# Sparse attention and a feed-forward layer on one core: batch 0's local q and k are cast and turned in halves, in a new order

## The chip, the cores and the metric

One core of a Trainium2 chip. The metric is the device time of one execution in microseconds (us). The kernel is bound to one core, so its time is that core's. Times inside the run are counted from the start of the profiled span.

## The reference

Eight batches of eight heads, 576 tokens, 64 numbers per head. Heads 0 to 3 attend to a local window of 32 earlier tokens, heads 4 to 7 to earlier tokens of the same residue modulo 32. The attention output, as 4608 rows of 512, goes through a feed-forward layer of width 2048 with a leaky slope of its own per column:

```python
rel = pos[:, None] - pos[None, :]
mask_local = (rel >= 0) & (rel < stride)          # stride = 32, heads 0..3
mask_strided = (rel >= 0) & (pos[None, :] % stride == pos[:, None] % stride)   # heads 4..7
attn = softmax(where(mask, q @ k.T / sqrt(D), -1e9))
x = (attn @ v).transpose(0, 2, 1, 3).reshape(B * S, H * D)
h = x @ w_in
out = (max(h, 0) + alpha * min(h, 0)) @ w_out
```

## The kernel before, in words

**Pairs.** Heads are worked on two at a time. A batch has four pairs: 0 and 1 are the local heads, 2 and 3 the strided heads; pair g of the whole run belongs to batch g // 4. For each pair the kernel computes scores (the two heads' 64 rows on the two halves of the partitions), exponentials on ScalarE, the product with v (which has a column of ones, so that the row sum comes with it), a reciprocal and a multiplication on VectorE, and transposes of the result into xT, the input of the first linear layer (line 585), which works on 512 tokens at a time in 16 pieces of 128 columns of w_in.

**Batch 0's stage.** Before line 585 can run at full length, batch 0's four pairs have to be through. This stage is written out by hand as a list of steps (lines 837 to 842), and `keep` holds every instruction in program order on its engine. The queues are in order: a step that waits holds back whatever stands behind it on the same engine. The steps:

- `warm(17)`, `w(1)`: matmuls of 512 columns on zeros, whose result nobody reads (lines 759 to 762).
- `F(nm, pr)` (`turn_first`, 146 to 158): the strided q or k of pair 2 + pr, as loaded, is transposed in two banks of four; ScalarE evicts the first, VectorE the second.
- `Sc(g, i)` (`score_piece`, 275 to 322): half i of pair g's scores, 6 or 8 short matmuls and two that add the mask, then the exponentials on ScalarE, in one instruction (i = 0, tile sp) or two (i = 1, two banks of tag "hps").
- `vs(0, pr)` (`cast_v`): VectorE copies the strided v of two heads into place. `alpha`: a small transpose and VectorE's 1 - alpha.
- `Cl(0, nm)` (`cast_l`, 177 to 180): POOL casts the local q or k (128 x 1152) from float32 to float16, all nine tokens of a partition at once.
- `T(0, nm)` (`transpose_piece`, 254 to 273): nine transposes into two banks (five and four tokens), each evicted into qT or kT: for q both by ScalarE, for k the second by VectorE.
- `Pv(g, a)` (`pv_piece`, 390 to 418): piece a of pair g's product with v, then a reciprocal (line 413) and a multiplication (line 415) on VectorE. A strided pair has three pieces (6, 6 and 4 blocks), a local pair two of 6.
- `X(g)` (`x_piece`, 428 to 440): pair g's result is transposed and evicted into xT, by ScalarE for a strided pair and VectorE for a local one, if nothing else is said.
- `ov(0, eng, c0, c1)` (`over_v`): copies the 32 rows of overlap in the local v, half on POOL, half on VectorE; the local Pv read them.
- `L(m)` (`lin1_piece` with `begin`, 573 to 590): the first two of the four matmuls of piece m of line 585, those that need pairs 2 and 3 only.

After the list come loads for batch 1, issued on POOL's and SP's queues, and the loop over the 16 pieces of line 585 (854 to 858); pieces 0 to 3, which were begun, need only the matmuls for pairs 0 and 1.

**Buffers.** PSUM has three buffers of tag "ps" (used by F, alpha, T, Pv and X in turn, and by some pieces of line 585), three of tag "hps" (one holds the warm matmuls' result until the last of them, the others serve the scores and line 585), and the two banks of sp. A buffer is free again when its last reader is done.

Of the kernel before, what the change touches and what calls it, by code (L numbers as in the profile page):

```python
# [10 lines left out]
F16 = mybir.dt.float16  # L11
# [21 lines left out]
def kernel(  # L33
# [10 lines left out]
    nc = tc.nc  # L44
    keep = tc.keep_in_program_order
# [11 lines left out]
    hpool = ctx.enter_context(tc.tile_pool(name="half", bufs=4))  # L57
# [5 lines left out]
    pspool = ctx.enter_context(tc.tile_pool(name="ps", bufs=3, space=bass.MemoryType.PSUM))  # L63
# [10 lines left out]
    ident = consts[:, 0:128]  # L74
# [10 lines left out]
    qTs = [cpool.tile([128, 2, 672], F16, name=f"qT{i}") for i in range(2)]  # L85
    kTs = [cpool.tile([128, 2, 672], F16, name=f"kT{i}") for i in range(2)]
# [7 lines left out]
    loaded = {}  # L94
    cast16 = {}
# [50 lines left out]
    def turn_first(nm, pr):  # L146

        t32 = loaded[(nm, pr)]
        dst = (qTs if nm == "q" else kTs)[1].rearrange("r e c -> r (e c)")
        for h in range(2):  # L150
            tp = pspool.tile([128, 512], F32, tag="ps", name="tf")
            for j in range(4):
                keep(nc.tensor.transpose(
                    tp[:, 72 * j : 72 * j + 72], t32[:, 512 * h + 128 * j : 512 * h + 128 * j + 128], id32))
            c0 = 320 * (2 * pr + h)
            cast_copy(("act", "dve")[h],
                      dst[:, c0 : c0 + 320].rearrange("r (j p) -> r j p", p=80)[:, :, 0:72],
                      tp[:, 0:288].rearrange("r (j p) -> r j p", p=72))
# [18 lines left out]
    def cast_l(b, nm, eng="pool"):  # L177
        t16 = hpool.tile([128, 9, 2, 64], F16, tag=f"{nm}l16", bufs=2, name=f"{nm}l16")
        cast_copy(eng, t16, loaded[(b, False, nm)].rearrange("p f (t d) -> p t f d", t=9))
        cast16[(b, False, nm)] = t16  # L180

    def load_v(b, strided):


        if strided:
            st = spool.tile([128, 2048], F16, tag="v", bufs=2, name="stv")
            step = 2 if b == 0 else 4
            for h in range(0, 4, step):
                keep(nc.gpsimd.dma_start(
                    st[0:72, 512 * h : 512 * (h + step)].rearrange("p (h e) -> p h e", h=step),  # L190
                    v[b, 4 + h : 4 + h + step, :, :].rearrange("h (p t) d -> p h (t d)", t=8)))
            loaded[b] = st
        else:
            v16 = vls[b % 2]
            base = v[b, 0:1, 0:1, :]
            r0 = 32 if b < 2 else 0
            step = 12 if b == 0 else 24
            for c in range(0, 24, step):
                keep(nc.gpsimd.dma_start(
                    v16[r0:128, c : c + step, 0:64],  # L200
                    bass.AP(tensor=base.tensor, offset=base.offset + (96 * c - 32 + r0) * D,
                            ap=[[D, 128 - r0], [96 * D, step], [1, D]])))
            cast16[(b, False, "v")] = v16

    def cast_copy(eng, o, i):
        if eng == "act":
            keep(nc.scalar.copy(o, i))
        elif eng == "dve":
            keep(nc.vector.tensor_copy(o, i))
        else:  # L210
            keep(nc.gpsimd.tensor_copy(o, i))  # L211
# [42 lines left out]
    def transpose_piece(u, nm):  # L254

        b = u // 2  # L260
        early = b < NEARLY
        src = cast16[(b, False, nm)]
        dst = qTs[u % 2][:, :, 0:576] if nm == "q" else kTs[u % 2][:, :, 32:608]
        o = dst.rearrange("r e (p t) -> r e p t", t=9)
        tps = []
        for t0, t1 in ((0, 5), (5, 9)):
            tp = pspool.tile([128, 8, 64, 2], F16, tag="ps", name="tp")
            for t in range(t0, t1):
                keep(nc.tensor.transpose(
                    tp[:, t - t0].rearrange("r p e -> r (p e)"), src[:, t].rearrange("p f d -> p (f d)"), ident))  # L270
            tps.append(tp[:, 0 : t1 - t0].rearrange("r t p e -> r e p t"))
        cast_copy("act", o[:, :, :, 0:5], tps[0])
        cast_copy("dve" if early and (u or nm == "k") else "act", o[:, :, :, 5:9], tps[1])
# [116 lines left out]
    def pv_piece(P, a):  # L390
        while defer and any(P.et[z][0] is defer_et["et"] for z in P.et):
            defer.pop(0)()
        if P.x16 is None:
            if P.xd and P.strided:
                P.x16 = x16s
            else:
                P.x16 = xpool.tile([128, 1024], F16, tag="x16", name="x16")
        v16 = cast16[(P.b, P.strided, "v")]
        grp = P.pgroups[a]
        r = 72 if P.strided else 128  # L400
        pv = pspool.tile([128, 512], F32, tag="ps", name="pv")
        nb = 2 * len(grp)
        for x in range(nb):
            t, hh = grp[x // 2], x % 2
            et, c = P.et[(t, hh)]
            keep(nc.tensor.matmul(  # L406
                pv[:, 65 * x : 65 * x + 65], et[0:r, c : c + 128],
                v16[0:r, 2 * P.pr + hh, t, :] if P.strided else v16[:, 6 * (2 * P.pr + hh) + t, :],
                start=(x == 0), stop=(x == nb - 1), skip_group_check=True))
        w = P.w  # L410
        rc = rpool.tile([128, 8], F32, tag="rc", name="rc")
        pvv = pv[0:w, 0 : 65 * nb].rearrange("r (c e) -> r c e", e=65)
        keep(nc.vector.reciprocal(rc[0:w, 0:nb], pvv[:, :, 64]))  # L413
        c0 = 128 * grp[0]
        keep(nc.vector.tensor_tensor(  # L415
            P.x16[0:w, c0 : c0 + 64 * nb].rearrange("r (c e) -> r c e", e=64),
            pvv[:, :, 0:64],
            rc[0:w, 0:nb].unsqueeze(2).to_broadcast([w, nb, 64]), op=ALU.mult))
# [9 lines left out]
    def x_piece(P, eng):  # L428
        xp = pspool.tile([128, 1024], F16, tag="ps", name="xp")
        for t in range(P.n):  # L430
            keep(nc.tensor.transpose(  # L431
                xp[:, P.w * t : P.w * t + P.w], P.x16[0 : P.w, 128 * t : 128 * t + 128], ident[0 : P.w, 0 : P.w]))
        for s0, d0, w in spans(P.b, P.strided):
            o = xT[:, P.hp, d0 : d0 + w]
            if P.strided:
                cast_copy(
                    eng, o.rearrange("r (p t) -> r p t", t=8),
                    xp[:, 0:576].rearrange("r (t p) -> r p t", t=8)[:, s0 // 8 : (s0 + w) // 8, :])
            else:
                cast_copy(eng, o, xp[:, s0 : s0 + w])  # L440
# [24 lines left out]
    def T(u, nm):  # L465
        return lambda: transpose_piece(u, nm)

    def Sc(g, i):
        return lambda: score_piece(pairs[g], i)

    def Pv(g, i):
        return lambda: pv_piece(pairs[g], i)

    def X(g, eng=None):
        return lambda: x_piece(pairs[g], eng or ("act" if pairs[g].strided else "dve"))

    for g in range(7, npair + 2):
        c = g // 4
        a, p, t = g, g - 1, g + 1
# [279 lines left out]
    def warm(n):  # L759

        for _ in range(n):
            keep(nc.tensor.matmul(wps, wrm[:, 0:128], wrm, start=True, stop=True))  # L762
# [11 lines left out]
            name=nc.get_next_instruction_name(), act_func_set_id=6, ins=[], outs=[]  # L774
# [35 lines left out]
    def F(nm, pr):  # L810
        return lambda: turn_first(nm, pr)
# [6 lines left out]
    def vs(b, pr):  # L818
        return lambda: cast_v(b, pr, "dve")

    def Cl(b, nm, eng="pool"):
        return lambda: cast_l(b, nm, eng)

    def ov(b, eng, c0, c1):
        return lambda: over_v(b, eng, c0, c1)

    def w(n):
        return lambda: warm(n)

    def L(m):  # L830
        return lambda: lin1_piece(0, m, True)

    def G(nm, pr):
        return lambda: turn_second(nm, pr, "act" if nm == "q" else "dve")

    warm(17)
    for fn in [
        F("q", 0), w(1), F("k", 0), w(1), F("k", 1), Sc(2, 0), vs(0, 0), w(1), F("q", 1), Sc(2, 1), alpha, Pv(2, 0),
        Sc(3, 1), vs(0, 1), Cl(0, "q"), Cl(0, "k"), Pv(2, 2), Sc(3, 0), w(1), Pv(3, 2), T(0, "q"), Pv(3, 0), w(1),
        Pv(3, 1), w(1), T(0, "k"), X(3), w(1), Sc(0, 1), Pv(2, 1), Sc(0, 0), Sc(1, 1), ov(0, "dve", 12, 24),  # L840
        ov(0, "pool", 0, 12), Pv(0, 1), X(2), Pv(0, 0), Sc(1, 0), Pv(1, 1), L(1), X(0, "act"), Pv(1, 0), L(2), L(3),
        X(1), L(0)]:
        fn()
    load_d(1)
    load_v(1, True)
# [127 lines left out]
```

## Time and profile before

| | us |
|---|---|
| median of three runs | 300.84 (300.59 to 300.93) |
| profiled execution | 300.67 |
| its span | 298.9 |
| TensorE busy in the span | 292.9 |
| VectorE busy | 219.1 |
| ScalarE busy | 178.8 |
| POOL busy | 172.8 |
| granted clock, mean | 1.000 |

The profiled execution has its own time, somewhat below the median; its span runs from the first instruction to the last. The engine rows give busy time, not time on the path. In a timeline a line is: start, duration, engine, line of the kernel and operation, what it writes and reads with shapes, how often, and in brackets how long the engine had been idle and what released it. In a chain a line is: start, duration, engine, what it writes and where. Starts of neighbours on an engine can overlap by some hundredths, since an instruction begins while the one ahead drains.

### The profile page before, as it was taken

Reading aid. Unit: us, or ns where it says so; the run is one execution under the profiler, and the core shown is the slowest. Engines: PE = TensorE matmul, PEld = TensorE weight load, DVE = VectorE, ACT = ScalarE, POOL = GpSimd, SP = SyncE. Lnnn points to the kernel's source line nnn. Section 1 sums busy time; section 2 is a strip of 40 time slices with the busy share of each in tenths; the row PEclk is TensorE's granted clock in tenths of the full one; section 3 lists DMA queues with packets and bytes.
Section 4 is the critical chain, followed back from the end, with each engine's and each line's share of the span. In section 5 each row is a group of like instructions: output and inputs, shape, how many; then the busy total and the mean of one; then the engine's idle time right before and its main releaser. Section 6 shows DMA issues by size and latency. Waiting matters only on the chain.

```text
span 298.9 us, 6826 instructions
## 1 busy us (share of the span) xinstructions
PE 292.9 (98%) x2683; PEld 183.0 (61%) x2683; DVE 219.1 (73%) x408; ACT 178.8 (60%) x332; POOL 172.8 (58%) x160
## 2 busy tenths in 40 slices
PE   8999999999999999999999999999999999999995
PEld 3764555554545478646864687468745974784484
DVE  5677886668775897589848984898489958936852
ACT  1676755698457775776477646764676356516730
POOL 8362270049969998979897988495653405002300
PEclk9999999999999999999999999999999999999999
DMA  7999999999998969999989999955911040022004
GB/s 183 257 193 202 256 197 259 217 200 295 113 200 140 113 101 97 159 190 132 127 156 182 158 139 188 170 89 96 205 24 21 16 148 0 2 72 70 0 2 141
DMA packets 96977, 41.18 MB, mean 138 GB/s; under 512 B 75361, under 2 KB 93233, under 8 KB 96945
## 3 DMA queue, kind: packets, MB, share of 16 engines
q0 software_dynamic: 51008, 17.77, 60.7%
q1 hardware_dynamic: 45584, 22.32, 34.6%
q10 hardware_dynamic: 352, 0.66, 0.9%
q8 instruction: 21, 0.34, 0.5%
q14 instruction: 12, 0.09, 0.1%
HBM read 38.24 MB, written 9.44 MB: 160 GB/s over the span
## 4 chain that ended last, share of the span: by engine, by line
PE 82%; DVE 10%; ACT 3%; issue 3%; DVEq 0%; ACTq 0%
PE hps L585 37%; PE ops L720 18%; PE ops L624 5%; PE ops L710 4%; PE pv L406 4%; DVE gsum L654 2%; PE wps L762 2%; PE ops L876 2%; DVE gT L596 2%; DVE x L415 2%; PE sp L353 2%; DVE x16s L415 1%; ACT neg L593 1%; PE sph L353 1%; PE xp L431 1%
## 5 line engine op out<-in xcount | busy, mean ns | idle before, releaser
L585 PE MATMUL hps<-xT,win 128*128 128x512 f16 x576 | 131.9, 379 | 0.0
L596 DVE SCALAR_TENSOR_TENSOR gT<-neg,oma,hps 128x512 f16<-128x512 f32 x144 | 105.3, 744 | 36.1 <-ACT neg L593 28.1
L593 ACT ACTIVATE neg<-hps 128x512 f32<-128x512 f32 x144 | 85.8, 598 | 35.2 <-PE hps L585 33.0
L585 PEld LDWEIGHTS <-win 128*128 128x128 f16 x576 | 53.7, 98 | 58.9 <-issue 0.2
L654 POOL TENSOR_TENSOR gsum<-gT 128x1024 f16<-128x1024 f16 x14 | 29.7, 2123 | 41.7 <-DVE gT L596 36.7
L378 POOL TENSOR_TENSOR et<-et,consts 128x576 f16<-128x576 f16 (+1 forms) x24 | 35.5, 1481 | 30.2 <-ACT et L376 30.0
L720 PEld LDWEIGHTS <-gT 128*128 128x128 f16 x336 | 31.5, 98 | 5.4 <-issue 0.3
L415 DVE TENSOR_TENSOR x<-pv,rc 96x384 f16<-96x384 f32 (+2 forms) x62 | 33.0, 532 | 2.1
L385 POOL TENSOR_TENSOR et<-et,consts 128x576 f16<-128x576 f16 (+1 forms) x24 | 31.5, 1313 | 0.0
L406 PEld LDWEIGHTS <-et 72*128 72x128 f16 (+1 forms) x448 | 23.4, 98 | 11.5 <-issue 1.2
L720 PE MATMUL ops<-wout,gT 128*128 128x256 f16 x224 | 27.9, 272 | 0.1
L710 PE MATMUL ops<-wsum,gsum 128*128 128x256 f16 x216 | 26.6, 273 | 0.0
L376 ACT ACTIVATE et<-sp 128x576 f16<-128x576 f32 (+1 forms) x24 | 15.5, 645 | 17.1 <-PE sp L353 17.1
L720 PEld LDWEIGHTS <-gsum 128*128 128x128 f16 x224 | 20.9, 98 | 2.6
L710 PEld LDWEIGHTS <-gsum 128*128 128x128 f16 x224 | 20.8, 98 | 2.6
L413 DVE RECIPROCAL rc<-pv 96x6 f32<-96x6 f32 (+2 forms) x80 | 14.6, 183 | 10.6 <-PE pv L406 10.4
L211 POOL COPY vs<-stv 72x1024 f16<-72x1024 f16 x12 | 13.4, 1117 | 14.5 <-DMA stv<-in_v_dram 14.5
L665 DVE TENSOR_TENSOR osb<-ops,par 128x512 f32<-128x512 f32 (+1 forms) x14 | 9.4, 672 | 15.7 <-PE ops L720 8.2
L382 ACT ACTIVATE et<-sph 128x288 f16<-128x288 f32 (+1 forms) x48 | 18.8, 409 | 0.0
L663 ACT COPY osb<-ops 128x512 f32<-128x512 f32 x14 | 8.2, 587 | 16.7 <-PE ops L720 16.7
L624 PE MATMUL ops<-wout,gT 128*128 128x512 f16 x64 | 16.4, 379 | 0.0
L406 PE MATMUL pv<-vs,et 72*128 72x65 f16 x256 | 15.4, 193 | 0.7 <-DVE x L415 0.5
(107 smaller groups left out, 355.4 us busy)
## 6 DMA issues: line engine op xcount, KB each, us to landing
out_dram<-osb SPq DMA_DIRECT2D x35, 256.0 KB, 4.3
vl<-in_v_dram POOLq DMA_DIRECT2D x6, 384.0 KB, 9.0
win<-in_moe_w_in_dram POOLq DMA_DIRECT2D x4, 512.0 KB, 17.7
wout<-in_moe_w_out_dram POOLq DMA_DIRECT2D x4, 512.0 KB, 16.5
qsd<-in_q_dram POOLq DMA_DIRECT2D x7, 288.0 KB, 6.3
ksd<-in_k_dram POOLq DMA_DIRECT2D x7, 288.0 KB, 8.3
stv<-in_v_dram POOLq DMA_DIRECT2D x7, 288.0 KB, 8.0
ql<-in_q_dram SPq DMA_DIRECT2D x3, 576.0 KB, 6.9
```

The source lines that it names most:

```text
L378: keep(nc.gpsimd.tensor_tensor(mv, mv, m, op=ALU.mult))
L382: keep(nc.scalar.activation(ev[:, n * y : n * y + n], sps[y][0:r, 0:n], AF.Exp, scale=SCALE))
L385: keep(nc.gpsimd.tensor_tensor(mv, mv, m, op=ALU.mult))
L406: keep(nc.tensor.matmul(pv[:, 65 * x : 65 * x + 65], et[0:r, c : c + 128], v16[0:r, 2 * P.pr + hh, t, :] if P.strided else v16[:, 6 * (2 * ...
L415: keep(nc.vector.tensor_tensor(P.x16[0:w, c0 : c0 + 64 * nb].rearrange("r (c e) -> r c e", e=64), pvv[:, :, 0:64], rc[0:w, 0:nb].unsqueeze ...
L585: keep(nc.tensor.matmul(hps, win16[:, kk, 128 * m : 128 * m + 128], xT[:, kk, c0 : c0 + 512], start=(kk == 2), stop=(kk == 1)))
L593: keep(nc.scalar.activation(neg, hps, AF.Relu, scale=-1.0))
L596: keep(nc.vector.scalar_tensor_tensor(gTs[n][:, m, :], neg, oma[:, m : m + 1], hps, op0=ALU.mult, op1=ALU.add))
L624: keep(nc.tensor.matmul(ops, gTs[n][:, kf, 128 * mt : 128 * mt + 128], wout16[:, kf, :], start=(kf == 0), stop=(kf == 15)))
L654: keep((nc.vector if eng == "dve" else nc.gpsimd).tensor_tensor(gsum[i][:, hs], a, b, op=op))
L710: keep(nc.tensor.matmul(o, gsum[i][:, y, 128 * z : 128 * z + 128], wsum[i][:, y, :], start=(x == "5" and y == 0 and (z == 0 or alone)), st ...
L720: keep(nc.tensor.matmul(o, lhs(y), rhs(y), start=(first and y == 0), stop=(y == 7), skip_group_check=True))
```

## The change

`cast_h` and `turn_h` are new. `cast_h(nm, h, eng)` casts half h of batch 0's local q or k (h = 0: tokens 0 to 4 of each partition's nine; h = 1: tokens 5 to 8), on the engine that is named; `turn_h(nm, h, eng)` transposes these tokens into one bank and evicts it. In the list they stand in place of `Cl(0, ...)` and `T(0, ...)`: q's second half is cast and turned before its first, three of the four half casts are on POOL and k's second is on ScalarE; of the evictions only k's second is on VectorE, as it was. The whole order of batch 0's list is new: F("k", 0) is ahead of F("q", 0); Sc(2, 1) ahead of F("q", 1); Pv(2, 1) stands ahead of the q and k turns, and Pv(3, 0) behind them; X(3) is evicted by VectorE instead of ScalarE, and so is X(0); the local scores come in another order, as do X(1), X(0) and the L pieces; there are ten single warm matmuls in place of seven. The rest of the kernel is the same.

```diff
+    def cast_h(nm, h, eng):
+
+        if (0, False, nm) not in cast16:
+            cast16[(0, False, nm)] = hpool.tile(
+                [128, 9, 2, 64], F16, tag=f"{nm}l16", bufs=2, name=f"{nm}l16")
+        t0, t1 = ((0, 5), (5, 9))[h]
+        cast_copy(eng, cast16[(0, False, nm)][:, t0:t1], loaded[(0, False, nm)].rearrange(
+            "p f (t d) -> p t f d", t=9)[:, t0:t1])
+
+    def turn_h(nm, h, eng):
+
+        t0, t1 = ((0, 5), (5, 9))[h]
+        dst = qTs[0][:, :, 0:576] if nm == "q" else kTs[0][:, :, 32:608]
+        tp = pspool.tile([128, 8, 64, 2], F16, tag="ps", name="tp")
+        for t in range(t0, t1):
+            keep(nc.tensor.transpose(
+                tp[:, t - t0].rearrange("r p e -> r (p e)"),
+                cast16[(0, False, nm)][:, t].rearrange("p f d -> p (f d)"), ident))
+        cast_copy(eng, dst.rearrange("r e (p t) -> r e p t", t=9)[:, :, :, t0:t1],
+                  tp[:, 0 : t1 - t0].rearrange("r t p e -> r e p t"))
...
+    def Ch(eng, nm, h):
+        return lambda: cast_h(nm, h, eng)
+
+    def Th(nm, h, eng):
+        return lambda: turn_h(nm, h, eng)
+
     warm(17)
     for fn in [
-        F("q", 0), w(1), F("k", 0), w(1), F("k", 1), Sc(2, 0), vs(0, 0), w(1), F("q", 1), Sc(2, 1), alpha, Pv(2, 0),
-        Sc(3, 1), vs(0, 1), Cl(0, "q"), Cl(0, "k"), Pv(2, 2), Sc(3, 0), w(1), Pv(3, 2), T(0, "q"), Pv(3, 0), w(1),
-        Pv(3, 1), w(1), T(0, "k"), X(3), w(1), Sc(0, 1), Pv(2, 1), Sc(0, 0), Sc(1, 1), ov(0, "dve", 12, 24),
-        ov(0, "pool", 0, 12), Pv(0, 1), X(2), Pv(0, 0), Sc(1, 0), Pv(1, 1), L(1), X(0, "act"), Pv(1, 0), L(2), L(3),
-        X(1), L(0)]:
+        F("k", 0), w(1), F("q", 0), w(1), F("k", 1), Sc(2, 0), Ch("pool", "q", 1), Ch("pool", "q", 0), Ch("pool", "k", 0),
+        Sc(2, 1), w(1), F("q", 1), vs(0, 0), alpha, w(1), Sc(3, 0), Pv(2, 0), Pv(2, 1), Sc(3, 1), w(1), Th("q", 1, "act"),
+        vs(0, 1), Pv(2, 2), w(1), Th("q", 0, "act"), Pv(3, 2), w(1), Pv(3, 1), w(1), Ch("act", "k", 1), Th("k", 0, "act"),
+        Th("k", 1, "dve"), w(1), X(2), Pv(3, 0), w(1), Sc(0, 0), Sc(1, 1), X(3, "dve"), ov(0, "pool", 0, 12),
+        ov(0, "dve", 12, 24), Sc(1, 0), Pv(0, 0), Sc(0, 1), Pv(1, 1), Pv(1, 0), L(2), Pv(0, 1), L(3), L(1), X(1), X(0), L(0)]:
         fn()
```

## The prediction

> **What bounds the kernel now.** I read the page first, then the chain of waits, then the timelines of single engines from 7 to 26 us. All times are us from the start of the span. The page's engine line and the engine shares of its chain:
>
> ```profile
> PE 292.9 (98%) x2683; PEld 183.0 (61%) x2683; DVE 219.1 (73%) x408; ACT 178.8 (60%) x332; POOL 172.8 (58%) x160
> ...
> PE 82%; DVE 10%; ACT 3%; issue 3%; DVEq 0%; ACTq 0%
> ```
>
> TensorE is the bound over the whole run, so a change in batch 0's hand-written stage is worth what it does to one moment: when the first full run of line 585 begins. The chain of waits through that stage:
>
> ```profile
> 15.16 0.20 DVE rc L413
> 15.38 0.55 DVE x L415
> 15.94 0.11 DVE rc L413
> 16.05 0.02 issue
> 16.07 0.56 DVE x L415
> ...
> 22.66 0.43 PE xp L431 x6
> 23.09 10.85 PE hps L585 x50
> ```
>
> From 15 to 16.7 us it is VectorE that leads; from 17 us on TensorE, without a gap, and from 23.09 us 50 matmuls of line 585 follow one another. Two of these belong to L(0) (22.93 to 23.36 on TensorE's timeline), so the loop's own first piece begins at 23.36. Later the chain has no DMA in it, and no TensorE wait on a DMA shows in the list of waits: **a delay at 23.36 goes through to the end.** Later VectorE and ScalarE parts of the chain (35 to 46 us) start from TensorE's results and move with it.
>
> VectorE's timeline of this stage has the rows that price nearly everything:
>
> ```profile
> 12.66 0.88 DVE L209 COPY vs<-stv 72x1024 f16<-72x1024 f16 x1
> ...
> 15.16 0.19 DVE L413 RECIPROCAL rc<-pv 72x6 f32<-72x6 f32 x1 [0.53 <-PE pv L406]
> 15.38 0.55 DVE L415 TENSOR_TENSOR x<-pv,rc 72x384 f16<-72x384 f32 x1
> 15.86 0.18 DVE L413 RECIPROCAL rc<-pv 72x6 f32<-72x6 f32 x1
> 16.07 0.55 DVE L415 TENSOR_TENSOR x<-pv,rc 72x384 f16<-72x384 f32 x1
> 16.55 0.71 DVE L209 COPY kT<-tp 128x512 f16<-128x512 f16 x1
> ...
> 23.13 0.46 DVE L209 COPY xT<-xp 128x576 f16<-128x576 f16 x1 [0.52 <-PE xp L431]
> ```
>
> One Pv of six blocks costs VectorE 0.70 from start to start (15.16 to 15.86), one of four 0.55 (13.47 to 14.01). The second k eviction ends at 17.26, and the first local score follows at 17.41. A second VectorE window (46 to 60 us) prices a strided pair's X there, and POOL's timeline the whole casts:
>
> ```profile
> 46.93 0.76 DVE L209 COPY xT<-xp 128x576 f16<-128x576 f16 x1
> ```
>
> ```profile
> 12.12 1.14 POOL L211 CAST ql<-ql 128x1152 f16<-128x1152 f32 x1 [3.92 <-DMA ql<-in_q_dram]
> 14.03 1.15 POOL L211 CAST kl<-kl 128x1152 f16<-128x1152 f32 x1 [0.77 <-DMA kl<-in_k_dram]
> ```
>
> **What is removed, added, moved.** Two whole casts on POOL become three half casts there (0.99 ns per element: 0.51, 0.64, 0.64) and one of 512 elements on ScalarE. No row has that form; it lies between 0.40 (288 from PSUM) and 1.15 (all 1152 on ScalarE, later in the run). I take 0.60, the 128x512 f32 row of line 593. The 18 transposes and four evictions (0.75 for five tokens, 0.72 for four) stay. Three 512-column warm matmuls are added, 0.22 each. Pv(2,1) moves ahead of the k turn, Pv(3,0) behind it. X(3) and X(0) leave ScalarE (0.64 each) for VectorE, at 0.76 (strided) and 0.46. POOL's DMA issues stay behind the over_v copy, which waits for the v load until 16.06 in both orders, so no load moves.
>
> **The walk through the new order**, each engine in program order, with a wait of 0.05 from one engine to another, and three buffers for tag "ps", each free only when the tile three earlier has been read. TensorE's issue costs from its timeline: F 0.51, warm 0.22, score 0.58 when a score follows and 0.49 otherwise, Pv 0.18, four or five transposes 0.22 or 0.28, X 0.26, two matmuls of line 585 0.43; results come 0.17 after the last issue.
> - F(k,0), F(q,0), F(k,1) and Sc(2,0) keep their times (7.46 to 10.0). Sc(2,1) comes at 10.09, F(q,1) at 10.80. ScalarE must do the exponentials of pair 2 first (to 11.57), so its q eviction ends at 11.96 and Sc(3,0) starts at 12.00. The extra warm ahead is hidden there.
> - vs(0,0) now stands behind that eviction on VectorE: 11.93 to 12.36. Pv(2,0) issues at 12.58 (11.57 before), and VectorE has Pv(2,0) and Pv(2,1) from 12.97 to 14.44.
> - vs(0,1): behind them, from 14.37, beside POOL's k cast (14.03 to 14.70). The 0.88 row ended 0.28 after such a cast (13.26 to 13.54), so 14.98 (14.80 unhindered).
> - VectorE then works without a pause: Pv(2,2) 14.91, Pv(3,2) 15.48, Pv(3,1) 16.02 to 16.79. On ScalarE the q halves are evicted by 15.70, the k half cast runs to 16.22, the first k half is evicted at 17.24. The second, on VectorE, is behind Pv(3,1): 16.74 to **17.45**, against 17.26. The half casts on POOL are over a microsecond earlier than needed: what they gain is lost in the two queues.
> - X(2), Pv(3,0) (its buffer is free at 17.24) and a warm end at 17.69, so Sc(0,0) starts there, against 17.41 for Sc(0,1) before. The last warm is thus 0.2 on the path; the others lie in waits for buffers.
> - Sc(0,0), Sc(1,1), X(3): transposed by 19.28. VectorE now carries the tail alone: X(3) 19.31 to 20.07, over_v from 20.00, then four Pv of 0.70 from 20.29, the last x ending at 23.16. TensorE's L pieces and X(1) fit between. X(0) needs that last x: transposes 23.21, results 23.64, eviction on VectorE 23.66 to 24.12. L(0) ends at 23.90, and the loop's first matmul needs X(0): **24.17** against 23.36.
>
> The sum is **+0.81**. VectorE's surplus, 0.76 + 0.46, explains it: before, ScalarE did both evictions while VectorE was at the Pv. The profiled execution took 300.67 with a span of 298.9; so 301.48 by it. The median of the runs, 300.84, is 0.17 above, which gives 301.65. I forecast 301.6.
>
> Bounds: scores packed at 0.49 and vs(0,1) unhindered take 0.4 off; a ScalarE half cast of 1.15 adds 0.3, a hindered vs(0,0) 0.3. The forecast's own range is +0.4 to +1.4: 301.2 to 302.2.
>
> **A rule weighed.** VectorE's copy of vs took 0.43 with POOL idle (10.22) and 0.88 under a POOL cast (12.66). The Trainium skill, page "SBUF — State Buffer", section "Who interferes with whom", says that VectorE's fast copies and GpSimd share a port pair which the first to start holds for its whole instruction. By it, vs(0,0) at 11.93 would go ahead of the cast at 12.12 and cost 0.43, as the sum has it. If the q load landed 0.2 sooner the cast would be first and the sum +1.1. The trace agrees for the second copy; no row here shows a cast held up by a copy.
>
> **Rivals.**
> 1. *The halves bring the local scores forward (faster).* The k load is there at 14.03; a half cast of 0.64, transposes of 0.45 and the 0.77 eviction could end at 16.0, and scores start at 16.1, 1.3 before 17.41. With a tail as long as now (17.41 to 23.36) the run ends 1.3 sooner: 299.5. It decides if VectorE reaches its k eviction by 16.0 and the tail is not VectorE's. Against it: five Pv and vs(0,1) stand ahead there (3.8 of work after 12.97). Even with every wait in the scores taken out I get no lower than 23.2, which is 300.7. Chance 0.12.
> 2. *No change.* The delay is made up later by loads that land at fixed times. POOL's cast of batch 1's q waits for its load until 39.22, and if this chain bounded TensorE a shift of 0.8 would vanish: 300.8. Against it: that cast is done at 40.47 and its transposes come at 43.31, behind Pv. It needs other slack, or scores and copies all at their cheap ends together. Chance 0.25.
> 3. *TensorE's clock falls.* The first warm matmuls come 0.43 apart until 6.3 and 0.22 after. Were the slow pace to come back for some 4 us in the stage's waits, line 585 would lose about 2: 303.5. The waits that I find are below 0.5, like those of before. With other unforeseen waits above +1.6: chance 0.08.
>
> **How the numbers follow.** The forecast has 0.55, the rivals 0.12, 0.25 and 0.08. The range 300.4 to 302.4 leaves out the first and the last, 0.20. A measurement of this kernel can tell 0.2%, or 0.6 us. Of the forecast's 0.55, 0.08 lies at +0.4 to +0.6 and counts as no change: faster 0.12, within 0.33, slower 0.55.
>
> **What would show it.** In the changed profile: the second k eviction on VectorE ends near 17.45, and Pv(3,1) ends just ahead of it; vs(0,0) takes about 0.43 and vs(0,1) 0.6; the first local score is near 17.7; VectorE has no pause from X(3) on, and X(3) takes 0.76 there; ScalarE is idle before the first neg; TensorE waits for X(0) and starts the loop near 24.2. If the k eviction ended by 16.5, or VectorE had gaps over 0.5 after X(3), the forecast would be wrong; so too if line 585 began at 24.2 and the end did not move.

## The result, and the profile after

The changed kernel takes 301.57 us (median of 21 runs, 300.96 to 302.03), the kernel before 300.70 in the same comparison: a ratio of 1.0024 (95% interval 1.0016 to 1.0031), or +0.72 us (+0.5 to +0.9). Forecast were 301.6 and a sum of +0.81.

New lines stand ahead of most of the kernel, so line 585 is now 606, line 415 is 436, line 413 is 434, and an eviction on ScalarE or VectorE is 228 or 230. The profiled execution took 301.34, with a span of 299.5. The engine line and the engine shares of its page:

```profile
PE 293.4 (98%) x2686; PEld 183.2 (61%) x2686; DVE 220.9 (74%) x410; ACT 178.1 (59%) x331; POOL 172.4 (58%) x161
...
PE 82%; DVE 11%; ACT 3%; issue 3%; DVEq 0%; ACTq 0%
```

TensorE is the bound as before; VectorE has a hundredth more of the chain. Where that lies shows in the chain of waits through the end of batch 0's stage (start, duration, engine, what it writes):

```profile
18.84 0.28 PE xp L452 x8
19.12 0.02 issue
19.14 0.06 DVE xT L230
19.20 0.73 issue
19.93 0.35 DVE vl L230
...
22.50 0.56 DVE x L436
23.06 0.05 issue
23.11 0.44 PE xp L452 x6
23.55 0.02 issue
23.57 0.47 DVE xT L230
24.05 0.04 issue
24.09 10.52 PE hps L606 x48
```

Before, the chain from 17 us on was TensorE's alone. Now it goes onto VectorE at 19.14, with X(3), and comes back only at 24.09, behind X(0)'s eviction (the 0.73 of "issue" is the time of X(3)'s copy, whose row follows). The loop's first piece starts 0.73 later than before, and the chain's later parts have moved by about as much (0.66 at 35 us and at the end). VectorE's timeline:

```profile
13.94 0.88 DVE L230 COPY vs<-stv 72x1024 f16<-72x1024 f16 x1
...
16.53 0.72 DVE L230 COPY kT<-tp 128x512 f16<-128x512 f16 x1
...
19.14 0.76 DVE L230 COPY xT<-xp 128x576 f16<-128x576 f16 x1 [0.87 <-PE xp L452]
...
23.06 0.97 DVE L230 COPY xT<-xp 128x576 f16<-128x576 f16 x2
```

The k eviction ends at 17.25, where it ended before (17.26), although POOL finished its first half cast of k at 14.53, and not at 15.18. From X(3) on VectorE has no pause.

### The profile page after: what moved, and what is told of

Same layout as the page of the kernel before. It is cut to its first block, busy times and chain, and to the rows that moved or that the text cites. A ratio compares the mean times of both kernels' runs of the same rounds, so it can differ in the third digit from the quotient of the medians.

```text
span 299.5 us, 6837 instructions
## 1 busy us (share of the span) xinstructions
PE 293.4 (98%) x2686; PEld 183.2 (61%) x2686; DVE 220.9 (74%) x410; ACT 178.1 (59%) x331; POOL 172.4 (58%) x161
## 4 chain that ended last, share of the span: by engine, by line
PE 82%; DVE 11%; ACT 3%; issue 3%; DVEq 0%; ACTq 0%
PE hps L606 37%; PE ops L741 18%; PE ops L645 5%; PE ops L731 4%; PE pv L427 4%; PE wps L783 3%; DVE gsum L675 2%; DVE x L436 2%; PE ops L903 2%; DVE gT L617 2%; PE sp L374 2%; DVE x16s L436 1%; ACT neg L614 1%; PE sph L374 1%; PE xp L452 1%
```

## The experiments

My theory: the halves gain nothing, since the queues that the k turn stands in come to it no sooner; the loss is VectorE's tail and one warm matmul, and it goes through to the end. Rivals: the halves do bring the scores forward; a delay is made up by later loads; TensorE's clock falls.

Eleven kernels, each timed beside the kernel before. The table gives the ratio and, from one profiled execution each, the start of the first F and of the first gT on VectorE, which follows the loop's first piece.

| | ratio to before (95%) | us by it | first F | first gT |
|---|---|---|---|---|
| before | 1 | 0 | 7.46 | 24.68 |
| changed | 1.0024 (1.0016 to 1.0031) | +0.72 | 7.09 | 25.35 |
| e1, delay of four matmuls | 1.0035 (1.0023 to 1.0048) | +1.05 | 7.12 | 25.55 |
| e2, halves in the old order | 1.0000 (0.9991 to 1.0009) | 0.0 | 7.12 | 24.40 |
| e3, X(3) on ScalarE | 1.0017 (1.0008 to 1.0026) | +0.51 | 7.24 | 25.16 |
| e4, and pairs exchanged | 1.0006 (0.9998 to 1.0015) | +0.18 | 7.11 | 24.75 |
| e5, whole casts in the new order | 1.0044 (1.0030 to 1.0058) | +1.32 | 7.08 | 25.88 |
| e6, one warm matmul less | 1.0018 (1.0010 to 1.0027) | +0.54 | 7.11 | 24.92 |
| e7, vs(0,1) earlier | 1.0030 (1.0018 to 1.0042) | +0.90 | 7.15 | 25.45 |
| e8, k turned early | 0.9989 (0.9980 to 0.9997) | -0.33 | 7.84 | 24.59 |
| e9, three losses undone | 0.9998 (0.9985 to 1.0011) | -0.06 | 7.40 | 24.94 |
| e10, e8 with whole casts | 0.9995 (0.9980 to 1.0010) | -0.15 | 7.27 | 24.30 |
| e11, no single warm matmuls | 1.0074 (1.0049 to 1.0100) | +2.2 | 7.48 | 27.20 |

The first F starts anywhere from 7.08 to 7.84, in kernels that up to there differ only in whether q or k comes first: it waits for the last of the 17 warm matmuls (the kernel before, 7.46) or for VectorE's cast of the identity matrix, which a small load feeds (e8, 7.84). The local k lands so that POOL's cast starts between 13.55 and 14.38. Hence times inside single executions are good to some 0.3. The length of the stage (first gT less first F) takes out the start of the first F, but not the landing of k.

**e1: does a delay go through?** The kernel before, with

```diff
-        X(1), L(0)]:
+        X(1), w(4), L(0)]:
```

> The kernel before, with four more single warm matmuls between X(1) and L(0), so that TensorE comes to the loop's first piece 4 x 0.22 = 0.88 us later and nothing else moves. If a delay at that moment goes through to the end (my step), the time is 0.88 us longer, about 301.6 against 300.7, and the second chain of waits has its parts 0.9 later throughout. If it is made up later by loads that land at fixed times (rival 2), the time stays within 0.2 us of the kernel before.

It took 301.68, +1.05 by the ratio. In the trace L(0) starts at 23.86 where the X(1) transposes end at 22.78: 1.08 later, 0.2 more than four matmuls; it starts 0.05 after the last warm result is complete (23.81), so it probably waits for the buffer that this result held. So 1.08 put in gave 1.05 (0.7 to 1.4) at the end: nothing is made up later, and rival 2 falls. The traces of the other kernels agree wherever the loop starts later than in the kernel before: the first gT against its 24.68, and the execution's own time against its 300.67, moved alike within 0.06 (the changed kernel by 0.67 and 0.67, e5 by 1.20 and 1.21). Where the loop starts sooner, in e2, e8 and e10, 0.1 to 0.7 of that was lost again; see e8.

**e2: the halves alone**, in the order before:

```diff
-        Sc(3, 1), vs(0, 1), Cl(0, "q"), Cl(0, "k"), Pv(2, 2), Sc(3, 0), w(1), Pv(3, 2), T(0, "q"), Pv(3, 0), w(1),
-        Pv(3, 1), w(1), T(0, "k"), X(3), ...
+        Sc(3, 1), vs(0, 1), Ch("pool", "q", 0), Ch("pool", "q", 1), Ch("pool", "k", 0), Pv(2, 2), Sc(3, 0), w(1), Pv(3, 2),
+        Th("q", 0, "act"), Th("q", 1, "act"), Pv(3, 0), w(1),
+        Pv(3, 1), w(1), Ch("act", "k", 1), Th("k", 0, "act"), Th("k", 1, "dve"), X(3), ...
```

> The kernel before in its old order, with the half casts and half turns alone: q's halves and k's first on POOL, k's second on ScalarE ahead of the k turn. My theory: the k cast ends sooner, but TensorE reaches the k turn only at 15.6 us and ScalarE is busy with q's evictions until then, so the second k eviction ends within 0.2 us of 17.26 and the time is within 0.3 us of the kernel before. Rival 1 (halves bring the local scores forward): the k eviction ends at 16.0 to 16.6 and the time is 0.7 to 1.3 us shorter.

No difference: a ratio of 1.0000 (the medians are 300.48 and 300.71). The last k eviction on its VectorE:

```profile
16.26 0.72 DVE L230 COPY kT<-tp 128x512 f16<-128x512 f16 x1
```

It ends 9.86 after the first F (16.98 less 7.12), before it was 9.80 (17.26 less 7.46). Rival 1 falls for this order: cast halves do nothing where TensorE comes to the turn later than the whole cast ends.

**e3 and e4: the tail.** The changed kernel with `X(3, "act")`, and then pairs 0 and 1 exchanged as well:

```diff
-        Sc(0, 0), Sc(1, 1), X(3, "dve"), ov(0, "pool", 0, 12), ov(0, "dve", 12, 24),
-        Sc(1, 0), Pv(0, 0), Sc(0, 1), Pv(1, 1), Pv(1, 0), L(2), Pv(0, 1), L(3), L(1), X(1), X(0), L(0)]:
+        Sc(1, 0), Sc(0, 1), X(3, "act"), ov(0, "pool", 0, 12), ov(0, "dve", 12, 24),
+        Sc(0, 0), Pv(1, 0), Sc(1, 1), Pv(0, 1), Pv(0, 0), L(2), Pv(1, 1), L(3), L(1), X(0), X(1), L(0)]:
```

> The changed kernel with X(3) evicted by ScalarE as before. If VectorE carries the tail (my theory), over_v and the four local Pv on VectorE start some 0.3 us sooner (near 19.9), but ScalarE's eviction pushes the last exponentials 0.25 to 0.3 later, so the last x ends near 22.9 instead of 23.05 and the time is 0.2 us shorter than the changed kernel's (0.1 to 0.3). If VectorE does not bound the tail, no difference at all, or longer by the exponentials' delay, 0.3.

> As the kernel with X(3) on ScalarE, and pairs 0 and 1 exchanged in the tail, so that pair 1's X is the last. The loop's pieces use pair 0 first and pair 1 one matmul (0.22 us) later. If the loop waits for the last eviction (my theory), this saves 0.22 us more: 0.4 us shorter than the changed kernel, some 0.3 to 0.4 longer than the kernel before. If the loop does not wait for it, no difference to the run with X(3) on ScalarE alone.

e3 is 0.2 below the changed kernel, as expected (the intervals overlap; the trace has the last x end at 22.86 in place of 23.05 although its first F is 0.15 later). e4 is 0.33 below e3, where 0.22 was expected; these intervals overlap too, but the traces have the 0.22: from the end of the last x to the first gT it is 2.30 in the changed kernel and in e3, 2.08 in e4 and in the kernel before. VectorE's last evictions in e4:

```profile
22.68 0.97 DVE L230 COPY xT<-xp 128x576 f16<-128x576 f16 x2
```

Both X(0) and X(1) are still on VectorE, back to back; but X(0) is first now and ends near 23.15, and X(1), which the loop needs one matmul later, at 23.65. So what costs is not that VectorE evicts X(0) but that the pair which the loop uses first comes last.

**e5: whole casts in the new order.** `Cl(0, "q"), Cl(0, "k")` in place of the three half casts on POOL, and ScalarE's half cast left out.

> The changed kernel with whole casts: POOL casts q and then k in one piece each at the same places, ScalarE's half cast of k goes, the turns stay in halves. If the halves themselves were worth something by bringing the cast forward (rival 1), q and k would be ready 0.5 us later and the time 0.3 to 0.5 longer than the changed kernel's only through TensorE's turns, with vs(0,1) unchanged at 0.88. My theory: TensorE comes to both turns later than the whole casts end (q 13.2 against 13.3, k 15.0 against 15.8), so the turns themselves lose nothing, but the longer k cast holds VectorE's vs(0,1) until 0.29 after it, 15.2 instead of 14.8, and with it VectorE's whole row up to the second k eviction: 0.4 us longer than the changed kernel, about 302.0. If copy and cast do not hinder one another, the same as the changed kernel.

It is 0.6 above the changed kernel (0.4 expected; the intervals barely overlap). vs(0,1) on VectorE and the k cast on POOL:

```profile
13.94 1.41 DVE L230 COPY vs<-stv 72x1024 f16<-72x1024 f16 x1
```

```profile
13.93 1.15 POOL L232 CAST kl<-kl 128x1152 f16<-128x1152 f32 x1 [0.58 <-DMA kl<-in_k_dram]
```

The copy, 0.42 when it meets no cast, ends at 15.35, which is 0.27 after the cast's end. In the changed kernel it ended 0.29 after the half cast's, in e6 0.28. TensorE's k turn (16.36) came 1.3 after the cast's end, and its q turn waited 0.06 at most. So in the new order the halves are worth 0.6, and all that the trace shows of it is a shorter hold on VectorE's copy: the second k eviction, further down VectorE's queue, ends at 17.79 in place of 17.25. The halves gain something here after all, though not because TensorE gets k sooner from the cast.

**e6 and e7: one wait each.** The changed kernel without the `w(1)` ahead of Sc(0,0); and with vs(0,1) between Pv(2,0) and Pv(2,1):

```diff
-        Pv(2, 0), Pv(2, 1), Sc(3, 1), w(1), Th("q", 1, "act"), vs(0, 1), Pv(2, 2), ...
+        Pv(2, 0), vs(0, 1), Pv(2, 1), Sc(3, 1), w(1), Th("q", 1, "act"), Pv(2, 2), ...
```

> The changed kernel without the single warm matmul between Pv(3,0) and Sc(0,0). My walk has this one on the path at 0.2 us: the first local score starts when the k eviction ends, near 17.35 instead of 17.6, and the time is 0.2 us shorter. If the warm matmul is covered by the wait for k, no difference.

> The changed kernel with vs(0,1) ahead of Pv(2,1), so that on VectorE it falls between POOL's q and k casts (13.25). By the row of 0.43 against 0.88 the copy takes 0.43, and Pv(2,2) to Pv(3,1) on VectorE come 0.3 to 0.45 sooner. But ScalarE's q eviction then waits for a buffer that Pv(2,1) holds longer, its k half cast ends 0.3 later, and the second k eviction is bound by that: k ready at 17.2 to 17.35 as now, first score 17.45 against 17.6, the time 0 to 0.2 us shorter than the changed kernel's. If VectorE's row alone set the k eviction, the time would be 0.4 shorter.

e6 is 0.18 below the changed kernel, as expected but within the intervals; in its trace the first score starts 0.05 after the second k eviction ends (17.18 against 17.13), in the changed kernel 0.36 after. e7 brought nothing (+0.90 against +0.72, within the intervals), and its ScalarE shows why:

```profile
15.05 0.75 ACT L228 COPY qT<-tp 128x640 f16<-128x640 f16 x1 [0.53 <-PE tp L197]
15.69 0.61 ACT L228 CAST kl<-kl 128x512 f16<-128x512 f32 x1
16.33 0.76 ACT L228 COPY kT<-tp 128x640 f16<-128x640 f16 x1
```

The vs copy took 0.47, but the transposes of q's first half waited 0.5 for a buffer. The trace names ScalarE's eviction ahead as the releaser; by the turn of the three buffers it is the one of Pv(2,1), whose x ended at 14.41, 0.16 before the transposes began (14.02 and 0.15 in the changed kernel). ScalarE then waited for them, and its cast of k's second half ended at 16.30 (15.89 in the changed kernel). The k eviction ended at 17.51. A wait was taken away and the next in line took its place.

**e9: the losses together.** e4 without the last warm matmul.

> The changed kernel with what the single runs priced put together: X(3) on ScalarE, pairs 0 and 1 exchanged in the tail, and no warm matmul ahead of the first local score. If the loss is these parts and they add up, the time is that of the kernel before, 300.7 to 300.9 (ratio 0.999 to 1.001). If something else in the new order costs time, it stays 0.4 us or more above.

300.83 against 300.84: the parts add up to the loss, and nothing else in the new order costs time that this comparison can tell, which is to within 0.4. In its trace the first score comes 10.23 after the first F (9.95 before) and the stage is 0.3 longer, so up to 0.3 may lie ahead of the scores still.

**e8 and e10: can the halves pay?** From the order before: all half casts on POOL, q's second half evicted by VectorE, both k evictions on ScalarE and ahead of Pv(3,0) and Pv(3,1), and Pv(2,1) and X(2) put into the waits before the scores. e10 has whole casts in it.

```diff
+        Sc(3, 1), vs(0, 1), Ch("pool", "q", 0), Ch("pool", "q", 1), Ch("pool", "k", 0), Ch("pool", "k", 1), Pv(2, 2),
+        Sc(3, 0), w(1), Pv(3, 2), Th("q", 0, "act"), Th("q", 1, "dve"), w(1), Th("k", 0, "act"), Pv(2, 1), w(1),
+        Th("k", 1, "act"), Pv(3, 0), X(2), w(1), Sc(0, 1), Pv(3, 1), Sc(0, 0), ov(0, "dve", 12, 24),
+        ov(0, "pool", 0, 12), Pv(0, 1), Sc(1, 1), X(3), Pv(0, 0), Sc(1, 0), Pv(1, 1), L(1), X(0, "act"), Pv(1, 0),
+        L(2), L(3), X(1), L(0)]:
```

> A version meant to beat both, from the order before: half casts all on POOL, q's second half evicted by VectorE, k's halves turned ahead of Pv(3,0) and Pv(3,1) with both evictions on ScalarE, Pv(2,1) and X(2) into the waits ahead of the local scores, the last pair still pair 1. By the walk k is ready at 16.7 (17.26 before), the first local score at 16.75 and the loop's first piece at 22.8 against 23.36: 0.5 us shorter than the kernel before, 300.2 (0.2 to 0.7). If the tail stays bound by VectorE and ScalarE however early the scores begin, no gain.

> The faster version (k turned early) with whole casts on POOL in place of its four half casts, the turns still in halves. There TensorE waited for the first k half cast, so the halves should count here: the k turn comes 0.4 us later, k is ready 0.2 to 0.4 later, and the time is 0.2 to 0.4 longer, close to the kernel before (300.6 to 300.8). If the gain came from the order alone, it stays at 300.4.

e8 beats both kernels, the kernel before by little: 300.36, a ratio of 0.9989 (0.9980 to 0.9997), or 0.33 where 0.5 was expected. TensorE's turn of k's first half there:

```profile
15.16 0.45 PE L197 MATMUL tp<-consts,kl 128*128 128x128 f16 x5 [0.17 <-POOL kl L232]
...
17.25 0.30 PE L316 MATMUL sph<-qT,kT 64*128 64x96 f16 x6
```

Here TensorE does wait for the cast, and the first local score comes 9.41 after the first F (9.95 before). The stage is 16.75 long against 17.22; with whole casts (e10) 17.03, and TensorE waits 0.46 for the cast. So by the traces, one execution each, the halves are 0.28 of e8's 0.47; the ratios of e8 and e10 overlap, so the times alone do not show it.

The profiled execution of e8 is itself no fast one: 301.24, the longest of its twelve, though its first gT came 0.09 sooner than before. By the trace it was lost in batch 1. VectorE's second pair of mask multiplications and POOL's cast of batch 1's q, in e8:

```profile
40.55 1.71 DVE L394 TENSOR_TENSOR et<-et,consts 72x576 f16<-72x576 f16 x2 [1.11 <-ACT et L388]
```

```profile
40.43 1.14 POOL L232 CAST ql<-ql 128x1152 f16<-128x1152 f32 x1 [6.94 <-DMA ql<-in_q_dram]
```

and in the kernel before, where the cast was over by then (39.22 to 40.47):

```profile
40.60 1.05 DVE L373 TENSOR_TENSOR et<-et,consts 72x576 f16<-72x576 f16 x2 [1.14 <-ACT et L367]
```

This pair takes 1.05 in every trace but three: 1.71 in e8, 1.28 in e2 and 1.26 in e10, the three in which the loop starts sooner than before and the cast runs beside the pair. So a late load can take back what the stage has gained, and in e8's trace took more than that.

**e11: no single warm matmuls** in the changed kernel.

> The changed kernel without any of its ten single warm matmuls (the 17 at the start stay). My prediction had only the last of them on the path: 0.2 us shorter, 301.3. Reading the trace after, the two between the first F steps (0.44) and those ahead of F(q,1) and Sc(3,0) also hold back the first exponentials and so VectorE's whole row up to the k eviction, which the loads allow some 0.6 to 1.1 us sooner: 300.5 to 301.0. If TensorE's clock falls without them (rival 3), matmuls of 512 columns are 0.43 apart for some microseconds and the time is 1 to 3 us longer.

It took 303.33. The busy times in stretches of 4 us (PE, PEld, DVE, ACT and POOL, with counts; then the mean granted clock and two columns on DMA):

```profile
12.00:16.00 4.00, 3.21 (x54) 2.42 (x53) 3.34 (x12) 3.33 (x7) 2.00 (x3) 1.00 1.93 205
16.00:20.00 4.00, 3.62 (x44) 2.38 (x46) 1.64 (x4) 2.60 (x5) 3.67 (x6) 0.59 1.25 199
20.00:24.00 4.00, 4.00 (x45) 2.59 (x45) 3.19 (x9) 1.40 (x4) 1.44 (x2) 0.55 1.24 205
```

The clock fell: two mask matmuls took 0.66 in place of 0.42. Seven of the eight runs have a mean granted clock of 0.976 to 0.989; the one with 1.000 took 300.86, 0.7 less than the changed kernel's median and within the 300.5 to 301.0 expected with the clock held. One run is no proof of that. That the clock falls in most runs without the warm matmuls is shown; that they always hold it is not: one of the 25 runs of the kernel before in this comparison, with its seven, has 0.989 too (302.58).

## Why the prediction was right

- **The time:** 301.6 against 301.57; the sum of 0.81 against 0.72 (0.5 to 0.9). That the time agrees better than the sum is luck: the kernel before is at 300.70 in this comparison, not at 300.84.
- **A delay goes through:** shown by e1 (1.08 in, 1.05 out). A gain goes through less surely (e8), which the prediction did not ask.
- **vs(0,0) behind the q eviction:** forecast 11.93 with the first F at 7.46; measured 11.57 with it at 7.09. It cost 0.42, ahead of the cast, as taken.
- **vs(0,1):** forecast end 14.98, measured 14.82. This was the main place where the early start of that execution was lost: the copy's end hangs on the k load, not on the first F.
- **The k eviction** 17.45 against 17.25, **the first score** 17.69 against 17.61, **the last x** 23.16 against 23.05, **the loop** 24.17 against 24.09. k landed sooner than taken (POOL's cast began at 13.81, not 14.03), and with vs(0,1) that is most of the 0.20 at the k eviction. Behind it the walk has slips of about 0.1 that cancel: the first score starts 0.10 after the end of the warm matmul ahead of it, where the walk has no gap; Sc(1,1) is counted at 0.58, though no score follows it and the walk's own price is then 0.49, as measured; over_v starts 0.79 after X(3), not 0.69. That the loop comes out within 0.1 is in part luck.
- **Half cast on ScalarE:** 0.60 taken from line 593, 0.61 measured; X(3) on VectorE 0.76, as taken. POOL's half casts, sized by elements at 0.51 and 0.64, took 0.61 and 0.71 to 0.72 (and 14.03 plus 0.64 is 14.67, not 14.70); this moves only the end of vs(0,1).
- **The halves' gain is lost in the two queues:** true of TensorE's turns (e2, e5), but not of VectorE. The walk itself lets the shorter cast free vs(0,1) sooner, and that is worth 0.6 (e5).
- **The last warm matmul:** 0.2 taken, 0.18 measured (e6), within the intervals.
- **VectorE's surplus of 0.76 + 0.46 explains it:** too simple. X(3) on VectorE is 0.2 (e3). X(0) on VectorE is free in e4, where the last xT eviction ends 0.98 after the last x (0.99 before); what is charged to it is the order of the last two pairs, 0.33 by the times and 0.22 by the traces (e4). The walk had that wait in it, the sentence that summed it up did not.
- **The other warm matmuls lie in waits:** not settled for each. e11 took all away and lost the clock, so it can't price them one by one.
- **Rival 3 by the waits that I found (below 0.5):** the clock did hold in this kernel, but not for that reason. In e11 no wait of TensorE is longer than 0.5 either, and the clock fell.

## What to carry to other kernels

An earlier result is worth something only if the engine that uses it comes to it sooner: ahead of splitting a step, look at what stands before its user in each queue, and at what else the longer step held up (0.6 in e5). In a hand-written order, let the last step be the one that the next stage needs last, and price an eviction's move by the chain it lands on, not by its duration. Matmuls that compute nothing can be load-bearing; take them away one at a time and look at the granted clock.

## What the runs showed of the hardware

- **TensorE's clock** had means of 0.59 and 0.55 in two stretches of 4 us in e11, with no idle stretch of TensorE over 0.5 us ahead of the fall; in 12 to 16 us it was busy 3.21 of 4, in the changed kernel 3.54, and there the clock held. The Trainium skill, page "TensorE: Matmul & The Clock Gate", section "Why this matters for your kernels", warns of idle gaps above about 3 us between bursts. By that row alone no gap here would count; in e11 leaving out ten matmuls of 0.22 was enough, so keeping to it is not enough in this kernel.
- **A VectorE copy and a POOL cast:** a vs copy that started while a cast ran ended 0.27 to 0.29 after that cast's end, whatever the cast's length (e5, the changed kernel, e6). The Trainium skill, page "SBUF — State Buffer", section "Who interferes with whom", has the one that starts second wait for the other's whole instruction; for the copy the traces agree, though what is left of it behind the cast is less than the 0.42 that it takes alone. The other way round they agree less: in e6 the cast of q's second half started 0.31 before a copy's end and took 0.77 in place of 0.61, so it lost 0.16 and not 0.31.
